# Transposing an expert tile's rows chunk by chunk, and cutting a scatter of rows into three pieces

## The chip, the cores and the metric

The kernel runs on one core of a Trainium2 chip. The metric is the device time of one execution in microseconds (us); lower is better. Each kernel is executed several times, and the median counts; one execution is also profiled, and all rows of the trace below come from that one.

## The reference

Three stages, all in float32, with batch 2, 8 heads, 576 positions, head size 64; 1152 tokens of 512 features; 8 experts of hidden size 1024; a last layer of hidden size 2048.

```
q_rot, k_rot = rotate(q), rotate(k)
attn = softmax(q_rot @ k_rot.T / 8)
x = (attn @ v) as [1152, 512]
logits = x @ w_gate + modality_bias[modality_id]
e_idx = argmax(logits);  gate_w = softmax(logits)[e_idx]
for e in range(8):
    mask = e_idx == e
    out[mask] = gate_w[mask] * (relu(x[mask] @ w1[e]) @ w2[e])
h = out @ w_in
out = (h * tanh(softplus(h))) @ w_out
```

## The kernel before, in words

**Products.** TensorE multiplies float32r operands. So that the result is as good as float32, each operand is kept as a high half (a rounded copy, made by ScalarE, ACT) and a low half (operand minus high half, made by VectorE, DVE, or GpSimd, POOL). Each product is three matmuls: high x high, high x low, low x high. For weights the halves are called `whi` and `wlo`, for tokens `xh` and `xl`, for the hidden layer `hh` and `hl`.

**Stages.** Attention fills the first 163 us. The expert stage follows up to 279 us, then the last layer. The batch has two halves, b = 0 and 1, of 576 tokens each. When attention for half b is done, `routing` (line 315) works out for each token its expert and its place among the rows sorted by expert. Then `scatters` (line 406) writes the half's rows from the tile `X` to `scratch` in DRAM: five indirect DMAs, one per tile of 128 (or 64) tokens, issued from POOL, each with a memset of a `spacer` behind it. Half 0's scatters are placed by a planner while attention still runs. Half 1's are issued in one go in the midst of its routing, since `routing` runs through them with `yield from scatters()` (line 422).

**Expert tiles.** The sorted rows of a half are worked off in tiles of T = 304 rows that belong to one expert: (0,0), (0,1), (1,0) and (1,1), with a loop for further tiles where an expert's rows don't fit, and which may run no times. `moe_tile` (line 681) handles one tile. Its weights come in eight chunks of 128 x 1024. `Feed.loads` (line 621) has SP load them ahead of use; `Feed.splits` (line 635) has ACT make a chunk's high half and POOL the low half, with a subtraction of about 2.4 us (line 611; chunk 4 of tile (0,0) goes to DVE). `Feed.ns` counts the chunks split so far. For f = 0 to 7, chunk f // 2 gives one block of the hidden layer with 12 matmuls; for d = 0 to 3, chunk 4 + d gives one block of the output with 24. The low halves of chunks 5, 6 and 7 of tile (0,0) appear in the trace as wlo(0, 0)_5, _6 and _7. The tags `whi` and `wlo` have three buffers each, so chunk n takes over that of chunk n - 3. A buffer of raw weights is free for SP's next load when POOL's subtraction has read it.

**Rows of the next tile.** At f = 3 SP loads the next tile's rows from `scratch`, as three row chunks of 128, 128 and 48 rows (`load_rows`, line 575); these loads wait until all scatters of their half have landed. At d = 0 ACT multiplies each row chunk by the gate (`moe_g`, line 645). Behind d = 1, `moe_x` (line 657) transposes the rows: for each of the four column chunks c it takes a PSUM bank, transposes the three row chunks into it, then ACT copies the bank to `xh` and DVE writes the difference to `xl`. Then the 48 matmuls of d = 2 and 3 follow, and the next tile. For tile (0,0) other code does this, inside attention (`x_tr`, line 1310), where the order is the planner's; `moe_x` serves tiles (0,1), (1,0) and (1,1). PSUM has seven banks in turn for this stage.

**The order of the work.** Each engine executes its own instructions in the order in which the program issues them, and this order is made by generators. `moe_tile` and what it calls yield a mark per instruction, with the engine's name and an estimated time. The loop at line 1473 runs half 1's routing and between its steps calls `pump` (line 1359), which advances the tiles by an allowance of TensorE's time; the allowance and two loads of the last layer's weights (`dl`) are chosen by the index of the routing's yield. Then `drive` (line 1451) runs the tiles on and, each 12 (later 7) yields of TensorE, issues one step of the decoding of the last layer's weights on DVE (lines 1401, 1406, 1411), up to a limit of 82 (72) steps.

```
        for i, y in enumerate(chain(route(1), merge_extra(nx))):
            if i in P["dl"]:
                dec_load(len(wr))
            if y[0] == "dve" or i == 8:
                pump(P["rq"][(i > 7) + (i > 8) + (i > 20)])
```

Of the kernel before, what the change touches and what calls it, by code (L numbers as in the profile page):

```python
# [10 lines left out]
F32 = mybir.dt.float32  # L11
F32R = mybir.dt.float32r
I32 = mybir.dt.int32
AF = mybir.ActivationFunctionType
ALU = mybir.AluOpType
# [10 lines left out]
T = 304  # L26
# [6 lines left out]
TCH = [(0, 128), (128, 128), (256, T - 256)]  # L33
KC = DM // 128
# [1 line left out]
FC2 = F2 // 128  # L36

Q = {'r0': 2.45, 'rd': 2.0, 'tanh': 1.06, 'rec': 1.1, 'hi': 2.2, 'lo': 2.38, 'o': 3.86}
P = {'sd': (4,), 'dl': (28, 44), 'qd': (2, 3), 'alt': (0.1, 4), 'd0': 82, 'vl': 24, 'w3': 3, 'rq': (0.2, 2.3, 0.55, 0.25), 'dec': (12, 7, 7), 'rl': 3, 'ah': 0, 'eps': 0.05, 'slack': 0.1}
K = {'ld': -22.67, 'prep': (-24.92, -22.38, -23.33, -27.14, -20.49, -7.62), 'sc': (-8.42, -3.18, 1.68, 1.67, 2.84, 10.44, 1.99, 8.05, 9.75), 'max': (-2.26, -5.46, -1.21, -1.85, 5.06, 8.41, 4.71, 11.42, 13.72), 'exp': (-3.19, 1.66, 6.32, 3.7, 13.26, 11.14, 14.6, -2.87, 25.74), 'tr': (0.69, 2.1, 2.56, 2.68, 5.53, 7.5, 8.45, 9.85, 10.88, 11.85, 15.56, 16.66, 16.92, 19.98), 'hi': (-3.91, -0.31, 2.51, 3.62, 4.25, 4.9, 5.01, 5.32, 7.26, 9.77, 13.56, 14.12, 14.6, 15.66), 'lo': (0.77, 1.83, 5.61, 6.34, 6.67, 7.32, 10.02, 10.73, 12.18, 13.92, 13.94, 14.62, 17.33, 18.02), 'pv': (7.08, 7.84, 10.5, 10.69, 14.13, 14.25, 14.32, 15.96, 18.04, 20.31, 21.03, 22.86, 23.97, 25.61), 'evac': (14.53, 9.65, 6.27, 25.13), 'rec': (-4.7, -0.45, 4.11, 12.71), 'fmm': (4.53, -3.79, 16.24, 17.22), 'norm': (15.5, 16.11, 26.18, 35.69)}  # L40

QT = [(0, 128), (128, 128), (256, 64), (320, 128), (448, 128)]
# [170 lines left out]
def moe_kernel(ctx: ExitStack, tc: tile.TileContext, aps, out):  # L213
    nc = tc.nc
# [95 lines left out]
    w4 = []  # L310
    tbl = {}
    scat, nxs, tes, tms = ([], []), [], [], []
    early = []

    def routing(b, bank):
        t = lambda sh, nm, dt=F32: rp.tile(sh, dt, tag=nm, name=f"{nm}{b}")
# [3 lines left out]
        def near(sh, nm):  # L320
# [19 lines left out]
            out=lg, in_=heads(X[b])[:, :, :, D:XW].rearrange("p j h e -> p j e h"),  # L340
# [15 lines left out]
            out=val, in0=lg, scalar=0.0, in1=iota8[:, 0:1, :].to_broadcast(sh),  # L356
# [12 lines left out]
        ps = bank()  # L369
# [5 lines left out]
        def scan():  # L375
# [8 lines left out]
            out=base[:, 1:], data0=ps[:, 0:n], data1=zero[:, :n],  # L384
# [8 lines left out]
            out=pos, in_=pz.rearrange("p (e j) -> p j e", j=5), axis=AX.X, op=ALU.add  # L393
# [9 lines left out]
        yield "dve", 0.12, True  # L403
        V.reciprocal(out=X[b][:, :, XC + 1], in_=sm8)

        def scatters():
            for j, (_, qn) in enumerate(QT):
                yield "pool", 1.25, False
                sc = nc.gpsimd.indirect_dma_start(
                    out=scratch,  # L410
                    out_offset=bass.IndirectOffsetOnAxis(ap=row[:qn, j:j + 1], axis=0),
                    in_=X[b][:qn, j], in_offset=None,
                )
                for o in scat[0] + scat[1]:
                    tc.declare_no_dep(sc.ins, o, reason="every token has a row of its own")
                for o in early if b else ():
                    tc.declare_no_dep(sc.ins, o, reason="rows of the other half")
                scat[b].append(sc.ins)
                nc.gpsimd.memset(spacer, 0.0)

        if b:
            yield from scatters()
        else:
            cur["scatters"] = scatters()
            yield "mark", 0.0, False
            side = False
# [11 lines left out]
            out=n1, in0=ce, scalar=float(T), in1=n0, op0=ALU.is_gt, op1=ALU.add  # L438
        )
        if side:  # L440
# [5 lines left out]
            out=qi, data0=n1, data1=zero[0:1, :NE], initial=0.0, op0=ALU.add, op1=ALU.add  # L446
# [7 lines left out]
            out=st, in0=s0, scalar=float(-T), in1=base[0:1, 0:n:5], op0=ALU.mult, op1=ALU.add  # L454
# [5 lines left out]
            out=nx, in0=qi[:, NE - 1:NE], scalar1=-2.0, scalar2=None, op0=ALU.add  # L460
        )
        tv = iotat[0:1, 0:ns]
        if b:
# [3 lines left out]
                out=tv[:, 0:2], in0=iotat[0:1, 0:2], scalar1=nx, scalar2=None, op0=ALU.add  # L467
# [3 lines left out]
                out=tv[:, 2:ns], in0=iotat[0:1, 2:ns], scalar1=nxs[0], scalar2=-2.0,  # L471
# [8 lines left out]
            out=lt, in0=qi[:, None, :].to_broadcast(s8),  # L480
            in1=tv[:, :, None].to_broadcast(s8), op=ALU.is_le,
# [9 lines left out]
            out=lt, in0=iota8[0:1, 0:1, :].to_broadcast(s8),  # L491
            in1=e8[:, :, None].to_broadcast(s8), op=ALU.is_equal,
# [8 lines left out]
            out=cs, in0=tv, scalar=float(T), in1=cs, op0=ALU.mult, op1=ALU.add  # L501
# [4 lines left out]
            out=tm[:, :, 1], in0=cs, scalar1=s1, scalar2=o1, op0=ALU.mult, op1=ALU.add  # L506
# [3 lines left out]
            out=tm[:, :, 1], in0=tm[:, :, 1], scalar1=0.0, scalar2=float(ROWS - T),  # L510
# [4 lines left out]
            out=tm[:, :, 0], in0=tm[:, :, 0], scalar1=float(NE - 1), scalar2=None, op0=ALU.min  # L515
# [98 lines left out]
    class Feed:  # L614
# [20 lines left out]
        def splits(self, n):  # L635
            while self.ns < min(n, self.nl):
                yield from split_chunk(*self.seq[self.ns])
                self.ns += 1
                yield from self.loads(0)

    xsplit, xpool = {}, []
# [15 lines left out]
    def moe_x(k, bank):  # L657

        if k not in gated:
            yield from moe_g(k)  # L660
        x = xrow.pop(k)
        pool = mp if k != "x" else xpool[0]
        xh = pool.tile([128, KC, T], F32R, tag="xh", name=f"xh{k}")
        xl = pool.tile([128, KC, T], F32R, tag="xl", name=f"xl{k}")
        for c in range(KC):
            yield "pe", 0.55, True
            ps = bank()
            for i, (r0, rn) in enumerate(TCH):
                nc.tensor.transpose(  # L669
                    out=ps[:, r0:r0 + rn], in_=x[:rn, i, c * 128:(c + 1) * 128],  # L670
                    identity=ident[:rn, :rn],
                )
            yield "act", 0.31, True
            nc.scalar.activation(out=xh[:, c], in_=ps[:, :T], func=AF.Copy)
            yield "dve", 0.39, True
            nc.vector.tensor_tensor(
                out=xl[:, c], in0=ps[:, :T], in1=xh[:, c].bitcast(F32), op=ALU.subtract
            )
        xsplit[k] = (xh, xl)

# [80 lines left out]
    def extra_tile(r):  # L761
# [4 lines left out]
        for _ in moe_x("x", cur["bank"]):  # L766
            pass
# [591 lines left out]
    def pump(x):  # L1359

        owed[0] += x
        while owed[0] > 0:
            y = next(gen0, None)
            if y is None:
                done0.append(1)
                return
            if y[0] == "pe":
                owed[0] -= y[1]
# [69 lines left out]
    with ExitStack() as mctx:  # L1438
# [34 lines left out]
        for i, y in enumerate(chain(route(1), merge_extra(nx))):  # L1473
            if i in P["dl"]:
                dec_load(len(wr))
            if y[0] == "dve" or i == 8:
                pump(P["rq"][(i > 7) + (i > 8) + (i > 20)])
        via[0] = cur["rtile"]
        drive(gen0, P["dec"][0], P["d0"], P["vl"])
        tile_rows(1)  # L1480
# [50 lines left out]
        def pool(name, bufs, **kw):  # L1531
# [4 lines left out]
        w2p, yp, gp, op = (  # L1536
            pool(n, b) for n, b in (("w2p", 1), ("yp", 1), ("gp", 3), ("op", 5))
        )
# [249 lines left out]
```

## Time and profile before

| what | us |
|---|---|
| median of three runs | 489.0 |
| the three runs | 492.23, 489.0, 488.71 |
| the profiled execution | 488.63 |
| its span, first to last instruction | 486.9 |

The span is what the trace covers; 1.7 us lie around it. In the rows, PE is TensorE's matmul, PEld its weight load, SPq the queue of SyncE, which issues most DMAs. A timeline row gives the start, the duration, the engine, the line, the operation with output and inputs, and the number of instructions in one row; in brackets the idle time of the engine before it and what ended it. Matmuls overlap: their durations are longer than the distance between their starts, and it is the starts that tell the pace.

### The profile page before, as it was taken

The numbers are of one execution on the slowest core, as the hardware profiler recorded it, in microseconds if no ns is written. First come the engines' busy times: TensorE is split into PE (matmuls) and PEld (weight loads), VectorE is DVE, ScalarE is ACT, GpSimd is POOL, SyncE is SP. The second block draws the span as 40 slices with busy tenths as digits, with TensorE's granted clock in tenths as the row PEclk, the third lists the DMA queues.
The fourth block names the chain that finished last, engine by engine and source line by source line (L and its number), as shares of the span: only waits on it lengthen the run. The fifth ranks groups of instructions, "written<-read, shape, count | busy, mean of one in ns | idle before, by whom it ended". The sixth has DMA issues, their size and how long they took to land.

```text
span 486.9 us, 8783 instructions
## 1 busy us (share of the span) xinstructions
PE 466.0 (96%) x2996; PEld 428.0 (88%) x2996; DVE 389.1 (80%) x616; ACT 332.5 (68%) x753; POOL 361.8 (74%) x363
## 2 busy tenths in 40 slices
PE   2799999999999989999999999999999999999995
PEld 1699999999989989999999998898989887888894
DVE  6698898899898665553878689999999859777773
ACT  3598888778878564574555487666676688776763
POOL 3799999999971697757756377877886749987654
PEclk9999999999999999999999999999999999999999
DMA  6789985877664598887974510012000001100002
GB/s 223 173 203 235 227 239 144 208 195 183 165 182 145 174 392 338 304 317 226 396 273 164 174 41 1 26 63 87 1 0 1 1 1 43 44 22 1 1 0 88
DMA packets 24131, 69.41 MB, mean 143 GB/s; under 512 B 5522, under 2 KB 9810, under 8 KB 22034
## 3 DMA queue, kind: packets, MB, share of 16 engines
q1 hardware_dynamic: 21794, 63.16, 41.9%
q0 software_dynamic: 1456, 5.03, 2.6%
q10 hardware_dynamic: 832, 0.61, 0.5%
q8 instruction: 25, 0.41, 0.4%
q14 instruction: 24, 0.20, 0.1%
HBM read 49.08 MB, written 6.44 MB: 114 GB/s over the span
## 4 chain that ended last, share of the span: by engine, by line
PE 52%; POOL 0%; issue 0%; ACT 0%; POOLq 0%; DVE 0%
PE h L1581 21%; PE o L1642 20%; PE mm L705 11%; PE mm L669 0%; POOL out_dram L1652 0%; POOLq L1784 0%; ACT ot L1648 0%; DVE yl L1519 0%; ACT yh L1517 0%; ACT Y L755 0%; POOL spacer L1659 0%; POOLq L1652 0%
## 5 line engine op out<-in xcount | busy, mean ns | idle before, releaser
L1607 DVE RECIPROCAL ta<-ta 128x320 f32<-128x320 f32 (+1 forms) x64 | 124.6, 1947 | 22.3 <-ACT ta L1600 20.8
L1555 POOL TENSOR_TENSOR w2l<-wc,w2h 128x512 fp32r<-128x512 f32 x64 | 90.3, 1432 | 16.4 <-ACT w2h L1554 8.3
L1642 PE MATMUL o<-w2h,g 128*128 128x512 f32 x288 | 97.7, 395 | 0.0
L1625 POOL TENSOR_TENSOR g<-ta,g 128x320 fp32r<-128x320 f32 (+1 forms) x63 | 51.7, 826 | 27.7 <-ACT g L1619 21.0
L972 PE MATMUL sc<-sk,sq 128*128 128x288 f32 (+1 forms) x320 | 59.4, 315 | 11.5 <-ACT sk L901 7.6
L1581 PE MATMUL h<-yl,w2h 128*128 128x320 f32 (+2 forms) x204 | 66.9, 328 | 0.1
L1581 PE MATMUL h<-yh,w2h 128*128 128x320 f32 (+2 forms) x204 | 66.9, 328 | 0.0
L1581 PE MATMUL h<-yh,w2l 128*128 128x320 f32 (+2 forms) x204 | 66.8, 328 | 0.0
L1642 PEld LDWEIGHTS o<-w2h,g 128*128 128x128 f32 x288 | 54.0, 188 | 11.6 <-POOL g L1625 0.2
L1007 ACT ACTIVATE pexp<-sc,nm 128x576 f32<-128x576 f32 x72 | 53.3, 741 | 15.5 <-DVE nm L996 11.7
L1040 ACT ACTIVATE ph<-pt 128x512 fp32r<-128x512 f32 (+2 forms) x112 | 54.8, 509 | 13.0 <-PE pt L1020 12.1
L996 DVE TENSOR_REDUCE nm<-sc 128x1 f32<-128x576 f32 x72 | 53.6, 752 | 10.8 <-PE sc L972 6.6
L972 PEld LDWEIGHTS sc<-sk,sq 128*128 128x128 f32 (+1 forms) x320 | 46.6, 190 | 14.2 <-ACT sk L901 7.9
L1642 PE MATMUL o<-w2l,g 128*128 128x512 f32 x144 | 56.8, 394 | 0.0
L1020 PE MATMUL pt<-ident,pexp 128*128 128x128 f32 (+1 forms) x360 | 54.5, 275 | 0.7 <-DVE tbl L521 0.6
L1061 PE MATMUL av<-ph,vhl 128*128 128x256 f32 (+1 forms) x160 | 50.7, 333 | 0.0
L1046 DVE TENSOR_TENSOR pl<-pt,ph 128x512 fp32r<-128x512 f32 (+1 forms) x80 | 48.7, 627 | 2.0 <-ACT ph L1040 1.8
L1596 ACT ACTIVATE ta<-h 128x320 f32<-128x320 f32 (+1 forms) x64 | 25.6, 401 | 30.7 <-PE h L1581 28.8
L1020 PEld LDWEIGHTS pt<-ident,pexp 128*128 128x128 f32 (+1 forms) x360 | 41.7, 136 | 3.5 <-issue 0.8
L1581 PEld LDWEIGHTS h<-yl,w2h 128*128 128x128 f32 x204 | 38.3, 188 | 4.1 <-DVE yl L1519 0.4
L1581 PEld LDWEIGHTS h<-yh,w2h 128*128 128x128 f32 x204 | 38.3, 188 | 3.9 <-DVE ta L1608 0.2
L1581 PEld LDWEIGHTS h<-yh,w2l 128*128 128x128 f32 x204 | 38.4, 188 | 2.3
(448 smaller groups left out, 1196.1 us busy)
## 6 DMA issues: line engine op xcount, KB each, us to landing
wr<-in_wio_dram SPq DMA_DIRECT2D x16, 1024.0 KB, 5.3
wc<-in_w_dram SPq DMA_DIRECT2D x26, 512.0 KB, 5.3
xs<-in_qk_dram SPq DMA_DIRECT2D x15, 576.0 KB, 5.3
sk<-ab SPq DMA_DIRECT2D x30, 288.0 KB, 4.1
sq<-ab SPq DMA_DIRECT2D x30, 144.0 KB, 2.4
vraw<-in_v_dram SPq DMA_DIRECT2D x16, 160.0 KB, 4.0
scratch<-zero SPq DMA_DIRECT2D x12, 108.8 KB, 5.0
xrow(0, 0)_2295<-scratch SPq DMA_DIRECT2D x2, 290.0 KB, 3.0
```

The lines of the kernel that those rows point to most:

```text
L705: nc.tensor.matmul(ps[:, :T], lhsT=w, rhs=m, start=(n == 0), stop=(n == 3 * len(pairs) - 1))
L972: nc.tensor.matmul(t[:m, hf, :NC2], lhsT=sq[:, c:c + m], rhs=sk[:, z, hf * NC2:(hf + 1) * NC2], start=(z == 0), stop=(z == 1),)
L996: nc.vector.tensor_reduce(out=nm[n, j], in_=sc[n, j][:, :, :NC2], axis=AX.XY, op=ALU.max, negate=True)
L1007: nc.scalar.activation(out=pe, in_=sc.pop((n, j))[:, :, :NC2], func=AF.Exp, bias=nm.pop((n, j)), accum_out=st[n, hf][:, i:i + 1],)
L1020: nc.tensor.transpose(out=t[:kn, o:o + 128], in_=pexp[n, j][:, k0:k0 + kn], identity=ident)
L1040: nc.scalar.activation(out=block(ph, n, hf, kts, slice(0, kn)), in_=psum(n, hf, kts, kn), func=AF.Copy)
L1061: nc.tensor.matmul(av[n, hf][:, :u.nq], lhsT=vhl[n][:, kt].rearrange("p a d -> p (a d)"), rhs=src[:, kt, u.at:u.at + u.nq], start=(kt == 0 ...
L1555: nc.gpsimd.tensor_tensor(out=lo[:, cs], in0=w[:, cs], in1=hi[:, cs].bitcast(F32), op=ALU.subtract)
L1581: nc.tensor.matmul(ps[:, :w], lhsT=wt[:, c], rhs=m[y][:, c], start=(n == 0), stop=(n == 11))
L1607: nc.vector.reciprocal(out=ta, in_=ta)
L1625: eng.tensor_tensor(out=gt[q][1][:, o:o + w], in0=tas.pop((q, i))[:, :w], in1=gt[q][0][:, o:o + w].bitcast(F32), op=ALU.subtract,)
L1642: nc.tensor.matmul(acc[g, t], lhsT=a[:, s], rhs=b, start=(f == 0 and z == 0), stop=(f == FC2 - 1 and z == 2),)
```

## The change

Two parts. In `moe_x` the loops are turned: row chunk by row chunk, each transposed for all four column chunks into four banks, then the four copies and differences. And half 1's scatters are issued as 0 to 2 where they were, 3 when six chunks have been split (behind chunk 5 of tile (0,0)), 4 when seven have. The indices that count the routing's yields are lowered by two.

```diff
-P = {'sd': (4,), 'dl': (28, 44), ...
+P = {'sd': (4,), 'ls': (6, 7), 'dl': (26, 42), ...
...
-    early = []
+    early, late = [], []
...
-        def scatters():
-            for j, (_, qn) in enumerate(QT):
+        def scatters(js=range(5)):
+            for j in js:
+                qn = QT[j][1]
                 yield "pool", 1.25, False
...
         if b:
-            yield from scatters()
+            yield from scatters(range(3))
+            late.extend(scatters([j]) for j in (3, 4))
...
                 yield from split_chunk(*self.seq[self.ns])
                 self.ns += 1
+                if self.ns in P["ls"]:
+                    yield from late.pop(0)
                 yield from self.loads(0)
...
-        for c in range(KC):
-            yield "pe", 0.55, True
-            ps = bank()
-            for i, (r0, rn) in enumerate(TCH):
+        ps = []
+        for i, (r0, rn) in enumerate(TCH):
+            yield "pe", (0.8, 0.8, 0.6)[i], True
+            for c in range(KC):
+                if i == 0:
+                    ps.append(bank())
                 nc.tensor.transpose(
-                    out=ps[:, r0:r0 + rn], in_=x[:rn, i, c * 128:(c + 1) * 128],
+                    out=ps[c][:, r0:r0 + rn], in_=x[:rn, i, c * 128:(c + 1) * 128],
                     identity=ident[:rn, :rn],
                 )
+        for c in range(KC):
             yield "act", 0.31, True
-            nc.scalar.activation(out=xh[:, c], in_=ps[:, :T], func=AF.Copy)
+            nc.scalar.activation(out=xh[:, c], in_=ps[c][:, :T], func=AF.Copy)
             yield "dve", 0.39, True
             nc.vector.tensor_tensor(
-                out=xl[:, c], in0=ps[:, :T], in1=xh[:, c].bitcast(F32), op=ALU.subtract
+                out=xl[:, c], in0=ps[c][:, :T], in1=xh[:, c].bitcast(F32), op=ALU.subtract
             )
...
-                pump(P["rq"][(i > 7) + (i > 8) + (i > 20)])
+                pump(P["rq"][(i > 7) + (i > 8) + (i > 18)])
```

## Rows read from the trace of the kernel before

**Rows 1.** The page's table of busy time: us, share of the span, instructions.

```profile
PE 466.0 (96%) x2996; PEld 428.0 (88%) x2996; DVE 389.1 (80%) x616; ACT 332.5 (68%) x753; POOL 361.8 (74%) x363
```

**Rows 2.** Waits of TensorE, 163 to 280 us: total, times, longest (all there are).

```profile
PE mm L705 <- POOL wlo(0, 0)_5_2744 L611: 1.2, 1, 1.2
PE mm L705 <- PEq L1493: 0.3, 1, 0.3
```

**Rows 3.** Timeline of TensorE at the first matmuls of chunk 5, tile (0,0).

```profile
180.10 0.30 PE L705 MATMUL mm<-hh(0, 0)_2571,whi(0, 0)_5_2742 128*128 128x304 f32 x1
180.24 0.30 PE L705 MATMUL mm<-hl(0, 0)_2572,whi(0, 0)_5_2742 128*128 128x304 f32 x1
181.76 0.41 PE L705 MATMUL mm<-hh(0, 0)_2571,wlo(0, 0)_5_2744 128*128 128x304 f32 x1 [1.22 <-POOL wlo(0, 0)_5_2744 L611]
182.01 0.30 PE L705 MATMUL mm<-hh(0, 0)_2571,whi(0, 0)_5_2742 128*128 128x304 f32 x1
```

**Rows 4.** Timeline of POOL: first and last of five scatters, two memsets, then wlo_5.

```profile
172.24 1.96 POOL L409 DMA_INDIRECT scratch<-X,row  x1
...
176.72 0.09 POOL L419 MEMSET spacer<- 1x1 f32 x1
...
178.29 0.97 POOL L409 DMA_INDIRECT scratch<-X,row  x1 [0.23 <-issue]
179.26 0.09 POOL L419 MEMSET spacer<- 1x1 f32 x1
179.32 2.39 POOL L611 TENSOR_TENSOR wlo(0, 0)_5_2744<-wc,whi(0, 0)_5_2742 128x1024 fp32r<-128x1024 f32 x1
```

**Rows 5.** Transposes of moe_x on TensorE: timelines, tile (0,1); busy time of three tiles.

```profile
184.95 2.25 PE L669 MATMUL mm<-ident,xrow(0, 1)_2628 128*128 128x128 f32 x12
187.12 0.41 PE L705 MATMUL mm<-hh(0, 0)_2571,whi(0, 0)_6_2792 128*128 128x304 f32 x1
...
185.06 0.46 PE L669 MATMUL mm<-ident,xrow(0, 1)_2628 128*128 128x128 f32 x2
...
185.26 0.52 PE L669 MATMUL mm<-ident,xrow(0, 1)_2628 48*128 48x48 f32 x2
...
185.45 0.44 PE L669 MATMUL mm<-ident,xrow(0, 1)_2628 128*128 128x128 f32 x2
...
sum 7.50, PE 6.73 PEld 4.27; mean PE 2.24 PEld 1.42
```

**Rows 6.** Timeline of TensorE in attention: transposes of tile (0,0), each with its successor.

```profile
155.35 0.45 PE L1312 MATMUL sc<-ident,xg(0, 0)_2423 48*128 48x48 f32 x4
155.73 0.41 PE L1020 MATMUL pt<-ident,pexp 128*64 128x128 f32 x2
...
159.15 0.93 PE L1312 MATMUL sc<-ident,xg(0, 0)_2423 128*128 128x128 f32 x7
159.95 0.33 PE L1091 MATMUL xo<-mov,avt 128*128 128x72 f32 x1
```

**Rows 7.** Timeline of TensorE: first readers of wlo_7 and of xl(0,1).

```profile
190.85 0.30 PE L705 MATMUL mm<-hh(0, 0)_2571,wlo(0, 0)_7_2845 128*128 128x304 f32 x1
...
194.05 0.30 PE L705 MATMUL mm<-xl(0, 1)_2923,whi(0, 1)_0_2948 128*128 128x304 f32 x1
```

**Rows 8.** Timeline of DVE: first decoding step after its wait, then xl(0,1).

```profile
185.92 0.70 DVE L1401 TENSOR_SCALAR rt<-wr 128x512 int32<-128x512 int32 x1 [6.00 <-DMA wr<-in_wio_dram]
...
187.99 1.61 DVE L676 TENSOR_TENSOR xl(0, 1)_2923<-mm,xh(0, 1)_2922 128x304 fp32r<-128x304 f32 x4
```

**Rows 9.** Timeline of ACT: the gates of tile (1,0).

```profile
208.74 1.94 ACT L651 ACTIVATE xrow(1, 0)_3073<-xrow(1, 0)_3073 128x512 f32<-128x512 f32 x3
```

**Rows 10.** Timeline of SP (two rows); landing of half 1's five scatters.

```profile
182.11 0.45 SPq L1385 DMA_DIRECT2D wr<-in_wio_dram  x1
...
195.85 1.46 SPq L580 DMA_DIRECT2D xrow(1, 0)_3073<-scratch  x3
...
DMA to landing us min/median/max: 7.6/8.3/8.4
```

More of the change, by code (lines that the diff above doesn't have):

```diff
@@ L38 @@
 Q = {'r0': 2.45, 'rd': 2.0, 'tanh': 1.06, 'rec': 1.1, 'hi': 2.2, 'lo': 2.38, 'o': 3.86}
-P = {'sd': (4,), 'dl': (28, 44), 'qd': (2, 3), 'alt': (0.1, 4), 'd0': 82, 'vl': 24, 'w3': 3, 'rq': (0.2, 2.3, 0.55, 0.25), 'dec': (12, 7, 7), 'rl': 3, 'ah': 0, 'eps': 0.05, 'slack': 0.1}
+P = {'sd': (4,), 'ls': (6, 7), 'dl': (26, 42), 'qd': (2, 3), 'alt': (0.1, 4), 'd0': 82, 'vl': 24, 'w3': 3, 'rq': (0.2, 2.3, 0.55, 0.25), 'dec': (12, 7, 7), 'rl': 3, 'ah': 0, 'eps': 0.05, 'slack': 0.1}
 K = {'ld': -22.67, 'prep': (-24.92, -22.38, -23.33, -27.14, -20.49, -7.62), 'sc': (-8.42, -3.18, 1.68, 1.67, 2.84, 10.44, 1.99, 8.05, 9.75), 'max': (-2.26, -5.46, -1.21, -1.85, 5.06, 8.41, 4.71, 11.42, 13.72), 'exp': (-3.19, 1.66, 6.32, 3.7, 13.26, 11.14, 14.6, -2.87, 25.74), 'tr': (0.69, 2.1, 2.56, 2.68, 5.53, 7.5, 8.45, 9.85, 10.88, 11.85, 15.56, 16.66, 16.92, 19.98), 'hi': (-3.91, -0.31, 2.51, 3.62, 4.25, 4.9, 5.01, 5.32, 7.26, 9.77, 13.56, 14.12, 14.6, 15.66), 'lo': (0.77, 1.83, 5.61, 6.34, 6.67, 7.32, 10.02, 10.73, 12.18, 13.92, 13.94, 14.62, 17.33, 18.02), 'pv': (7.08, 7.84, 10.5, 10.69, 14.13, 14.25, 14.32, 15.96, 18.04, 20.31, 21.03, 22.86, 23.97, 25.61), 'evac': (14.53, 9.65, 6.27, 25.13), 'rec': (-4.7, -0.45, 4.11, 12.71), 'fmm': (4.53, -3.79, 16.24, 17.22), 'norm': (15.5, 16.11, 26.18, 35.69)}
```

## The prediction, made blind

> **What bounds the kernel now.** I read four views, from wide to narrow. First the page's table of busy time: TensorE is busy for 466.0 of 486.9 us [rows 1], so little can be won except by giving it less to do or by closing a gap in it. Then TensorE's waits in the expert stage, 163 to 280 us: there are two in the whole stage, 1.2 us for one low half of weights, wlo(0,0)_5, that POOL makes late, and 0.3 us at a branch [rows 2]. Then the timeline on both sides of the first wait. On TensorE the second matmul of chunk 5 starts at 180.24, the third only at 181.76 [rows 3]. On POOL the reason is in sight: five scatters of half 1 stand in one row from 172.24 to 179.35, and wlo(0,0)_5 is the next instruction behind them [rows 4]. Last, the transposes of a tile's rows: twelve of them hold TensorE from 184.95 to 187.12, 0.18 us each [rows 5], while the transposes of tile (0,0), which stand in the attention stage with their 48-row pieces together, go at less than that [rows 6]. So TensorE sets the end, and both parts of the change touch its own queue.
>
> **Part 1: the scatters in pieces.** Two ordinary matmuls of this shape start 0.14 us apart (180.10 and 180.24). Without the wait the third would stand at 180.38; it stands at 181.76, 1.38 us late, and the step behind it, to 182.01, is 0.25 instead of 0.14, another 0.11 [rows 3]. The pause therefore costs 1.49 us, not the 1.2 us of the waits view.
>
> After the change POOL issues scatters 0 to 2, then wlo_5, scatter 3, wlo_6, scatter 4, wlo_7. The memset behind scatter 2 ends at 176.81. wlo_5 starts at once (it followed the last memset so before) and takes 2.39 us: ready at 179.2 instead of 181.7 [rows 4]. Its high half is there: TensorE used it at 180.10 [rows 3]. TensorE asks at 180.38, so 1.2 us are to spare and the whole 1.49 us goes. What is late next? Scatter 3 starts some 0.2 us behind wlo_5 and takes 0.97 like the last one before; with its memset it ends at 180.5, so wlo_6 is ready at 182.9. Scatter 4 puts wlo_7 at 184.2 to 186.6 [rows 4]. TensorE read wlo_6 two matmuls behind 187.12 and wlo_7 at 190.85 [rows 5, 7]; less 1.49 and the 0.82 of part 2 that is 185.1 and 188.5. Both have about 2 us of cover. A scatter in this stretch took 0.97 to 1.96 us [rows 4]. With 1.96 for each late one, wlo_7 is ready at 188.6, a cost of 0.1 us at most. I take 0.97, since the 1.96 is one of five and stood beside a DVE subtraction, while DVE is idle from 179.92 to 185.92 [rows 8].
>
> What else moves: SP's next weight load waits for wlo_5 and stands in front of the second decoder load at 182.11 [rows 10]; both leave 2.5 us earlier. Scatters 3 and 4 end on POOL about 2.4 and 4.8 us later than before; they land 7.6 to 8.4 us after issue [rows 10], so the last row is in place near 192. The row load of tile (1,0) waits for it on SP; it ran at 195.85 [rows 10] and will be due near 193.5. That is 1.5 us of cover. Should it fail, the rows are wanted only by ACT's gates at 208.74 less 2.3 [rows 9], 13 us later; a landing as slow as the scatters' leaves another 4 us.
>
> The shifted indices (26, 42 and 18 for 28, 44 and 20) count two scatter yields less and name the same points of the routing: nothing.
>
> **Part 2: row chunk by row chunk.** The rows of narrow windows give the steps from one transpose's start to the next: 128 rows behind 128 rows 0.11 (184.95 to 185.06), 48 rows behind 128 0.20 (to 185.26), 128 behind 48 0.19 (to 185.45) [rows 5]. Four such groups make the 2.17 us. A change of the row count is what costs: eight of the twelve steps are such changes (the last one leads to the next matmul). The new order has eight pieces of 128 rows, then four of 48: two changes.
>
> The sum: seven steps of 0.11 are 0.77; one of 0.20; then four of 48 rows with the way out. The attention stage has just that: from 155.35 to the next instruction at 155.73, 0.38 us [rows 6]. It also has seven of 128 rows in 0.80 us, 0.114 a step. Together 1.35 instead of 2.17: 0.82 us saved per tile. Three tiles pass through this code, with twelve transposes and the same busy time each (6.73 us for three) [rows 5] ((0,0) is done by other code): 2.46 us.
>
> Bounds: if each 48-row step costs the 0.20 of a change, it is 0.77 + 0.80 + 0.19 = 1.76, a saving of 0.41 per tile, 1.2 in all. The new order also changes the PSUM bank at each step instead of each third. If that alone made every step 0.20, it would be 11 x 0.20 + 0.19 = 2.39, a loss of 0.22 per tile, 0.7 in all. The four of 155.35 also went to four banks, and took 0.38 us with the way out, so I take 0.82. Nothing speaks for less than 0.11 on the 128-row steps.
>
> The Trainium skill ("TensorE: Matmul & The Clock Gate", section LDWEIGHTS) says that a weight load's time goes by its columns, not its rows, so that a 32-row load lasts as long as a 128-row one, some 107 ns for 128 columns. By that the three steps among the 48-row pieces would be 0.107 us each, 0.13 us more per tile than the sum above has. The trace goes against it: four such pieces in 0.38 us with the way out [rows 6].
>
> The copies out of PSUM begin later: ACT's first behind the ninth transpose instead of the third, about 0.7 us, then four in a row. They and DVE's four differences are wanted by the next tile's first matmuls, 48 matmuls or 6.7 us behind the transposes; xl was started at 187.99 and read at 194.05 [rows 7, 8]. Four banks at once were also live before, out of seven; the fourth takes over the bank of a product evacuated long before. The function yields three times for TensorE instead of four, so the decoding steps on DVE, counted in such yields, slip by one to three matmuls (0.4 us); their number by the stage's end stays, since limits cap it. No matmul of this stage waits for DVE [rows 2], so: nothing.
>
> **The sum.** 1.49 + 2.46 = 3.95 us. The profiled execution took 488.63 with a span of 486.9; 488.63 - 3.95 = 484.7. The median shown is 489.0, 0.4 above that execution, so on its scale 485.0. Behind the expert stage TensorE runs without a gap that is not its own, so what is won there arrives at the end.
>
> **Rivals** (times on the median's scale, 489.0).
>
> A, the array's steps don't shrink as in the attention stage (bank changes or 48-row steps at the price of a change): between a loss of 0.7 and a gain of 1.2; with the pause closed that is 486.3 to 488.2, say 487.2. For it: the order in attention was not quite this one. Against: all kinds of step are in the rows.
>
> B, the pause only moves from wlo_5 to wlo_6 or wlo_7, since the late scatters run slow (1.96 and more): 489.0 - 2.46 = 486.5. It needs over 1 us per scatter beyond the usual.
>
> C, the 48-row pieces follow each other at the 0.11 of the 128-row ones, since both load 128 columns: 0.77 + 0.20 + 0.33 + 0.19 = 1.49 per tile, 3 x 0.14 = 0.4 us less gained, 485.4. Against it stands the row of four [rows 6]. (The rule of the page named above would lead here.)
>
> D, the other side: the loads that wlo_5 releases earlier collide with decoder weights already under way. DVE stands until 185.92 for these [rows 8], and the differences xl(0,1) stand behind its decoding. xl(0,1)'s first piece was begun at 187.99 [rows 8], so ready at 188.5; TensorE wanted it at 194.05 [rows 7] and will at 191.7. From 3.2 us of delay each further microsecond is TensorE's; over 3.2 + 3.95 = 7.2 us the kernel is slower than it was; with 9 us, half as much again as DVE's whole wait of 6.00, it is 485.0 + 5.8 = 490.8. Against: the bytes under way are the same, and two loads of 1.5 MB leaving 2.5 us earlier can hardly take more than about 1.2 us of the others' time (half of 2.5, an estimate).
>
> **How the numbers follow.** Chances: forecast 0.69, A 0.10, B 0.10, C 0.07, D 0.04. The forecast's own range is 484.2 to 486.0 (0.1 to 0.2% of scatter on such runs). The range reaches over C and B and half of A: 484.0 to 487.6. About 1%, 4.9 us, is what a measurement of this kernel can tell from no change. The forecast, 0.8%, lies short of it: faster by over 1% 0.20 (the runs' own scatter must help), within 1% 0.77, slower by over 1% (the far end of D) 0.03.
>
> **What would show it.** Right: TensorE's waits no longer name wlo(0,0)_5; POOL shows scatter, wlo_5, scatter, wlo_6, scatter, wlo_7; the twelve transposes take about 1.35 us to the next matmul, the 48-row ones four in a row; tile (1,0) starts about 3.1 us earlier, the first product of the last stage 3.9 us earlier. Wrong: a wait for wlo(0,0)_6 or _7 or for xl(0,1) on TensorE, transposes still over 1.8 us, an ACT gate that waits for rows, or an earlier start of the last stage that is lost again before the end.

## The result, and the profile after

The kernel after takes 485.3 us (median of six, 485.0 to 485.4) against 488.9 in the runs of before beside it: a ratio of 0.9916, interval 0.9892 to 0.9939. One of the six runs of before took 492.23 us, the others 488.71 to 489.25; by the medians alone the gain is 3.6 us and the ratio 0.9926. The forecast was 485.0 us. The profiled execution took 485.32 us with a span of 483.6, so 3.3 us less than the profiled one of before, where the sum had said 3.95. TensorE is busy 1.8 us less [rows 1], and of its waits in the expert stage the one for wlo(0,0)_5 is gone. The page's table of busy time, then TensorE's waits, 163 to 280 us as in [rows 2] (here from 155 on; the first row is attention's):

```profile
PE 464.2 (96%) x2996; PEld 427.7 (88%) x2996; DVE 390.4 (81%) x616; ACT 331.2 (68%) x753; POOL 361.9 (75%) x363
```

```profile
PE xo L1098 <- ACT avt L1077: 0.5, 1, 0.5
PE mm L712 <- PEq L1500: 0.3, 1, 0.3
```

(Lines stand one to seven further down in the kernel after: L409 is L410, L611 is L613, L669 is L675, L705 is L712.) POOL's timeline shows the order of the change. wlo_5 starts where the third scatter's memset ends; it is ready at 179.35, and TensorE uses it at 180.66, with no pause. POOL's rows, then TensorE's:

```profile
172.41 1.97 POOL L410 DMA_INDIRECT scratch<-X,row  x1 [0.15 <-issue]
...
175.97 0.92 POOL L410 DMA_INDIRECT scratch<-X,row  x1 [0.22 <-issue]
176.88 0.09 POOL L420 MEMSET spacer<- 1x1 f32 x1
176.94 2.41 POOL L613 TENSOR_TENSOR wlo(0, 0)_5_2740<-wc,whi(0, 0)_5_2738 128x1024 fp32r<-128x1024 f32 x1
179.51 0.99 POOL L410 DMA_INDIRECT scratch<-X,row  x1 [0.17 <-issue]
...
180.56 2.41 POOL L613 TENSOR_TENSOR wlo(0, 0)_6_2792<-wc,whi(0, 0)_6_2790 128x1024 fp32r<-128x1024 f32 x1
183.13 0.98 POOL L410 DMA_INDIRECT scratch<-X,row  x1 [0.17 <-issue]
...
184.18 2.39 POOL L613 TENSOR_TENSOR wlo(0, 0)_7_2845<-wc,whi(0, 0)_7_2843 128x1024 fp32r<-128x1024 f32 x1
```

```profile
180.52 0.30 PE L712 MATMUL mm<-hl(0, 0)_2572,whi(0, 0)_5_2738 128*128 128x304 f32 x1
180.66 0.31 PE L712 MATMUL mm<-hh(0, 0)_2571,wlo(0, 0)_5_2740 128*128 128x304 f32 x1
180.81 0.30 PE L712 MATMUL mm<-hh(0, 0)_2571,whi(0, 0)_5_2738 128*128 128x304 f32 x1
```

The transposes of tile (0,1) [rows 5] take 183.73 to 185.07, 1.34 us to the next matmul instead of 2.17. TensorE's timeline, with a row of a narrower window between, which shows the four 48-row pieces in one run:

```profile
183.73 1.41 PE L675 MATMUL mm<-ident,xrow(0, 1)_2628 128*128 128x128 f32 x12
...
184.69 0.45 PE L675 MATMUL mm<-ident,xrow(0, 1)_2628 48*128 48x48 f32 x4
...
185.07 0.41 PE L712 MATMUL mm<-hh(0, 0)_2571,whi(0, 0)_6_2790 128*128 128x304 f32 x1
```

Step by step, from the starts of the twelve in the trace: 128 rows behind 128 go at 0.109 us, the first 48-row piece follows at 0.203, the next three at 0.099, 0.061 and 0.063, and the matmul behind them at 0.153. All three tiles are alike; the windows view of line 675 (PE busy, its count, weight loads, clock, DMA share, GB/s):

```profile
183.73:185.06 1.33, 1.33 (x12) 1.12 (x11) 1.00 1.03 419
211.90:213.23 1.33, 1.33 (x12) 1.12 (x11) 1.00 1.10 431
240.60:241.93 1.33, 1.33 (x12) 1.12 (x11) 1.00 0.97 403
```

Where the time came from and where some went again is read best by stage: how long from the first matmul of the expert stage to the first transpose of tile (0,1), how long to the first product of the last layer, and from there to the end of the span. TensorE's timeline, first before, then after:

```profile
162.89 0.38 PE L705 MATMUL mm<-xh(0, 0)_2502,whi(0, 0)_0_2371 128*128 128x304 f32 x1
...
279.17 0.31 PE L1581 MATMUL h<-yh,w2h 128*128 128x320 f32 x1
```

```profile
163.17 0.39 PE L712 MATMUL mm<-xh(0, 0)_2502,whi(0, 0)_0_2371 128*128 128x304 f32 x1
...
275.45 0.31 PE L1588 MATMUL h<-yh,w2h 128*128 128x320 f32 x1
```

To the first transpose it is 22.06 us before and 20.55 after, 1.50 less, which is part 1. The whole expert stage is 116.28 before and 112.27 after, 4.01 less; of the other 2.51, the transposes of the three tiles make 2.49, which is part 2. From there to the end it is 207.74 before and 208.16 after, 0.42 more. And attention had let the stage begin 0.28 later. 4.01 - 0.42 - 0.28 = 3.31, the difference of the spans.

**The 0.42 us in the last layer.** TensorE stops there once, in front of the third product of line 1649. Counted from the layer's first product, the matmuls ahead of this one start as in the kernel before, within 0.06 us; this one starts 0.32 us later, the next 0.43, and nothing further is lost. The weight-load row of the kernel after, whose bracket names the wait, and around it TensorE's row:

```profile
356.52 0.40 PE L1649 MATMUL o<-w2l,g 128*128 128x512 f32 x1
357.07 0.73 PE L1649 MATMUL o<-w2h,g 128*128 128x512 f32 x2
...
357.07 0.30 PEld L1649 LDWEIGHTS o<-w2h,g 128*128 128x128 f32 x2 [0.58 <-POOL g L1632]
```

POOL's g (the last layer's activated hidden block) stands behind DVE's reciprocals, and DVE is busy for 51.28 of the 52 us from 305 to 357. What made DVE late lies at 331 us. The timelines of DVE and POOL there, before:

```profile
333.55 1.26 DVE L1728 CAST idi<-idf 128x9 int32<-128x9 f32 x1
334.72 1.21 DVE L1411 SCALAR_TENSOR_TENSOR wc<-wr,wc 128x1024 int32<-128x1024 int32 x1
335.86 2.14 DVE L1607 RECIPROCAL ta<-ta 128x320 f32<-128x320 f32 x1
...
333.48 3.61 POOL L1555 TENSOR_TENSOR w2l<-wc,w2h 128x512 fp32r<-128x512 f32 x2
```

and after:

```profile
329.82 1.26 DVE L1735 CAST idi<-idf 128x9 int32<-128x9 f32 x1
331.00 2.39 DVE L1418 SCALAR_TENSOR_TENSOR wc<-wr,wc 128x1024 int32<-128x1024 int32 x1
333.31 2.14 DVE L1614 RECIPROCAL ta<-ta 128x320 f32<-128x320 f32 x1
...
329.75 2.55 POOL L1562 TENSOR_TENSOR w2l<-wc,w2h 128x512 fp32r<-128x512 f32 x2
```

The reader is to see an exchange. The same decoding step takes 1.21 us before and 2.39 after. POOL's two subtractions beside it take 3.61 together before and 2.55 after. The cast in front, of nine elements a partition, takes 1.26 us in both: as long as POOL's first subtraction still runs. When that ends, DVE's step and POOL's second subtraction are both due (their starts in the trace are 12 ns apart before and 18 after), and one of the two takes a subtraction longer than the other. Before, this was POOL, which had slack; after, it was DVE, which had none. From this step on, counted again from the layer's first product, DVE's instructions start 1.18 to 1.19 us later than before, and POOL's from 336 us on 1.18 to 1.20, up to the g for which TensorE stops. The 1.18 us that DVE lost reach TensorE as this stop; the rest is cover that TensorE had, since before this g had ended 0.9 us ahead of the matmul that reads it. It is not the clock: from 305 to 357 us it was granted at 1.00 in both executions.

The Trainium skill ("SBUF — State Buffer", section Who interferes with whom) says that a DVE instruction with two SBUF inputs contends with a GpSimd instruction that reads SBUF, that the lock is exclusive, and that the order of issue decides who is blocked. The rows agree as to the lock (DVE's step 1.21 against 2.39 us, POOL's two subtractions 3.61 against 2.55). As to the order they show less: DVE's start is recorded first in both executions, and it lost in one.

### The profile page after: what moved, and what is told of

It reads as the page before. It is cut to its first block, busy times and chain, and to the rows that moved or that the text cites. A ratio compares the mean times of both kernels' runs of the same rounds, so it can differ in the third digit from the quotient of the medians.

```text
span 483.6 us, 8783 instructions
## 1 busy us (share of the span) xinstructions
PE 464.2 (96%) x2996; PEld 427.7 (88%) x2996; DVE 390.4 (81%) x616; ACT 331.2 (68%) x753; POOL 361.9 (75%) x363
## 4 chain that ended last, share of the span: by engine, by line
PE 41%; DVE 8%; issue 3%; POOL 1%; ACT 1%; POOLq 0%; DVEq 0%; ACTq 0%
PE h L1588 15%; PE o L1649 15%; PE mm L712 11%; DVE ta L1614 6%; DVE wc L1418 1%; DVE ta L1615 1%; POOL out_dram L1659 0%; DVE wc L1408 0%; PE mm L675 0%; DVE wc L1413 0%; POOLq L1791 0%; POOL g L1632 0%; DVE idi L1735 0%; ACT ot L1655 0%; DVE yl L1526 0%
## 5 line engine op out<-in xcount | busy, mean ns | idle before, releaser
L1562 POOL TENSOR_TENSOR w2l<-wc,w2h 128x512 fp32r<-128x512 f32 x64 | 89.3, 1417 | 15.3 <-ACT w2h L1561 15.3
L1632 POOL TENSOR_TENSOR g<-ta,g 128x320 fp32r<-128x320 f32 (+1 forms) x63 | 52.7, 841 | 27.9 <-ACT g L1626 21.3
L1626 ACT ACTIVATE g<-ta 128x320 fp32r<-128x320 f32 (+1 forms) x64 | 27.9, 436 | 22.9 <-DVE ta L1615 22.5
```

The costliest lines, as they stand in the source:

```text
L1562: nc.gpsimd.tensor_tensor(out=lo[:, cs], in0=w[:, cs], in1=hi[:, cs].bitcast(F32), op=ALU.subtract)
L1632: eng.tensor_tensor(out=gt[q][1][:, o:o + w], in0=tas.pop((q, i))[:, :w], in1=gt[q][0][:, o:o + w].bitcast(F32), op=ALU.subtract,)
```

## The experiments

Each kernel ran beside runs of the kernel before. Those beside the parts alone, the first profile of the mixed order and the cast moved in the kernel after had a median of 489.17 us, those beside the others 489.51, so the ratios are to be compared, not the times. The theory: the change's two parts add up by the prediction's sum (a pause of POOL's making, and a price for each change of the row count), and the 0.42 us come from the exchange between DVE and POOL. The rivals: the bank order or the pieces' size makes the transposes slow; the parts cover each other; the last layer loses because it begins earlier.

### One part alone

The order of the transposes alone (the kernel after, with all five scatters in a row and the indices as before):

```diff
-            yield from scatters(range(3))
-            late.extend(scatters([j]) for j in (3, 4))
+            yield from scatters()
```

> Only the new order of the transposes; half 1's five scatters in one row as before. My theory (the two parts are independent and add): the wait for wlo(0,0)_5 stays, 1.2 us in the waits view and 1.5 in all; the twelve transposes take 1.34 us to the next matmul instead of 2.17 at all three tiles; the last layer's first product starts 2.5 us earlier than before, and the time is 486.4. Rival (the parts overlap, one of them alone brings most): 485.3 to 485.8.

The scatters alone (the kernel after, with the loops of `moe_x` as before):

```diff
-        for i, (r0, rn) in enumerate(TCH):
-            yield "pe", (0.8, 0.8, 0.6)[i], True
-            for c in range(KC):
...
+        for c in range(KC):
+            yield "pe", 0.55, True
+            ps = bank()
+            for i, (r0, rn) in enumerate(TCH):
```

> Only the scatters in three pieces; the transposes column chunk by column chunk as before. My theory: no wait for wlo(0,0)_5 and none for _6 or _7; transposes 2.17 us; the last layer's first product 1.5 us earlier than before, time 487.4. Rival (the parts overlap): 485.3 to 486.

Measured: the order alone 486.59 us, ratio 0.9949 (0.9934 to 0.9963), which is 2.5 us; the scatters alone 487.7 us, ratio 0.9974 (0.9965 to 0.9984), 1.3 us. By the ratios the two make 3.8 and the whole change 4.1 (0.84%); by the medians it is 2.6 and 1.5 against 3.6. They add up as far as the intervals can tell, and neither came near the 485.3 to 486 of the rival. The expert stage tells it more finely (table below): 2.70 and 1.57 us shorter, 4.01 for the whole change, and 0.18 of the 2.70 belongs to a pause that was shorter in that execution. In the trace of the order alone the wait is back, in TensorE's waits and in its timeline:

```profile
PE mm L711 <- POOL wlo(0, 0)_5_2744 L612: 1.0, 1, 1.0
```

```profile
180.49 0.30 PE L711 MATMUL mm<-hh(0, 0)_2571,whi(0, 0)_5_2742 128*128 128x304 f32 x1
180.63 0.30 PE L711 MATMUL mm<-hl(0, 0)_2572,whi(0, 0)_5_2742 128*128 128x304 f32 x1
181.97 0.41 PE L711 MATMUL mm<-hh(0, 0)_2571,wlo(0, 0)_5_2744 128*128 128x304 f32 x1 [1.04 <-POOL wlo(0, 0)_5_2744 L612]
182.22 0.30 PE L711 MATMUL mm<-hh(0, 0)_2571,whi(0, 0)_5_2742 128*128 128x304 f32 x1
```

Here the pause costs (181.97 - 180.63 - 0.14) + (182.22 - 181.97 - 0.14) = 1.31 us, against 1.49 in [rows 3]: TensorE would have used wlo_5 at 180.77, 0.39 later than in [rows 3], and POOL began it at 179.53, only 0.21 later than in [rows 4]; 1.49 - 0.18 is the 1.31. So the term of part 1 is not a constant. It is what POOL is late by in an execution. The two timed kernels that have part 1 alone (the scatters alone, and the mixed order below) put it at 1.3 by their ratios, 1.4 to 1.5 by their medians.

### What makes a transpose slow

The kernel after, with the row chunks in turn, 128, 128, 48, and each transpose to another bank than the one before it:

```diff
-        for i, (r0, rn) in enumerate(TCH):
-            yield "pe", (0.8, 0.8, 0.6)[i], True
-            for c in range(KC):
...
+        ps = [bank() for _ in range(KC)]
+        for s in range(12):
+            if s % 4 == 0:
+                yield "pe", (0.8, 0.8, 0.6)[s // 4], True
+            c, i = s % KC, s % 3
```

> The changed kernel with the twelve transposes in another order: 128, 128, 48 rows in turn as before, but each into another bank than the one ahead of it. My theory (the change of the row count is the price, not the bank): 2.17 us to the next matmul, as before the change; time 1.49 below before, or 487.4 to 487.8. Rival (three transposes in one bank in a row are the price): 1.35 us as in the changed kernel, 485.3.

Measured, a single execution: 490.21 us, more than either expected value. The twelve transposes took 2.17 us at each tile, as the theory has it. But the expert stage had begun at 166.01, some 2.8 us later than in the kernel after. The reason stands in front of everything that was edited: POOL had waited 2.1 us for an input load, and behind it DVE and TensorE waited too. The two rows, POOL's and TensorE's timeline:

```profile
130.21 2.65 POOL L924 TENSOR_TENSOR xs<-xs,tabs 128x1152 f32<-128x1152 f32 x1 [2.06 <-DMA xs<-in_qk_dram]
...
135.67 0.55 PE L1027 MATMUL pt<-ident,pexp 128*128 128x128 f32 x3 [2.14 <-DVE pl L1053]
```

Whether the new order had brought this was to be settled by more executions of the same kernel.

> The same kernel as e4_mixed (128, 128 and 48 rows in turn, each transpose to the next bank), timed in rounds. In its one look the transposes took 2.17 us to the next matmul, as in the kernel before, but TensorE had also stood still for 2.1 us at 133 us, in the attention stage, for a DVE reciprocal behind an input load that landed late. Theory (only changes of the row count cost): this stop was of that execution alone; without it the kernel keeps part 1's gain and has nothing of part 2's: about 487.6 us (487.2 to 488.0), with 2.17 us at each of three tiles and no stop at 133 us. Rival (the mixed order itself moves the stage ahead of it and costs 2 us): 489.8 to 490.4 again, with the stop at 133 us there again.

Measured: 488.15 us (487.88 to 488.58), ratio 0.9973 (0.9963 to 0.9983), which is what the scatters alone gave (0.9974); on the scale of the first group that is 487.8. The stop at 133 us is not there. Of line 675 the windows view shows, tile by tile, the price of before:

```profile
184.33:186.49 2.16, 2.16 (x12) 1.28 (x11) 1.00 1.07 436
213.34:215.49 2.15, 2.15 (x12) 1.28 (x12) 1.00 1.00 411
242.87:245.03 2.16, 2.16 (x12) 1.28 (x11) 1.00 0.84 337
```

A new bank with each transpose costs as much as a new bank with each third one (2.17 us both), and nothing in the kernel after. What costs is a change between 128 and 48 rows. The step over it takes 0.19 to 0.20 us (0.15 where the four 48-row pieces lead to the next matmul), and the step behind it is longer too: 0.164 to 0.169 instead of 0.109 among 128-row pieces, 0.099 instead of 0.06 among 48-row ones. The old order and the mixed one have eight changes in twelve steps, the new one two. Two starts of tile (0,1) in the kernel before show such a step behind a change, from the 185.45 of [rows 5] to 185.62, and the next change:

```profile
185.62 0.27 PE L669 MATMUL mm<-ident,xrow(0, 1)_2628 128*128 128x128 f32 x1
...
185.82 0.26 PE L669 MATMUL mm<-ident,xrow(0, 1)_2628 48*128 48x48 f32 x1
```

TensorE's weight loads show where much of it goes. The loads of the 128-row pieces begin one piece ahead: in the kernel after, the first at 183.59 for its matmul at 183.73. The load of a 48-row piece behind a 128-row one begins only together with its own matmul, after 0.17 us without a load. Waits of the weight loads at these lines, 182 to 250 us, before, after and in the mixed order; then, of the kernel after, the loads of tile (0,1) as a group (shortest, median and longest in ns) and the four 48-row ones in the timeline:

```profile
PEld mm L669 <- issue: 2.0, 12, 0.2
```

```profile
PEld mm L675 <- issue: 0.5, 3, 0.2
```

```profile
PEld mm L675 <- issue: 2.0, 12, 0.2
```

```profile
L675 PEld LDWEIGHTS mm<-ident,xrow(0, 1)_2628 x12: 136/140/145, 183.6 to 184.9; 128*128 128x128 f32 x8, 48*128 48x128 f32 x4
```

```profile
184.69 0.32 PEld L675 LDWEIGHTS mm<-ident,xrow(0, 1)_2628 48*128 48x128 f32 x4 [0.17 <-issue]
```

The nine pauses that are gone are 1.5 of the 2.49 us of part 2. The Trainium skill ("TensorEngine Tiling (Array Packing)", section Key Properties) says that a change of the tiling mode drains TensorE. It gives no price, and whether going from 128 to 48 rows is such a change no row shows: the pauses would fit it, and the cause of the price stays open.

### How late POOL may be

The kernel after, with four scatters in front of wlo_5 and one behind it, and the indices that count the yields one higher:

```diff
-            yield from scatters(range(3))
-            late.extend(scatters([j]) for j in (3, 4))
+            yield from scatters(range(4))
+            late.extend(scatters([j]) for j in (4,))
```

> After, but with four scatters in a row ahead of wlo(0,0)_5 and only one behind it. One scatter with its memset takes 1.27 us on POOL, so wlo(0,0)_5 should start at about 178.2 instead of 176.94 us and be ready at 180.6; TensorE asks for it at about 180.8. Theory (the pause is what POOL is late by, with a threshold): no wait or at most 0.2 us, transposes at 1.34 us; the time of after, 485.3 us (485.0 to 485.7). Rival (each scatter that stands ahead costs its share of the pause, some 0.7 us for this one, since two of the five were moved for 1.49 us): a wait of about 0.7 us for wlo(0,0)_5 and 486.0 us.

Measured: 485.47 us, ratio 0.9915 (0.9898 to 0.9931), the time of after. The waits view names no wait for wlo(0,0)_5, and the steps in TensorE's timeline are 0.18 and 0.24 around the matmul that asks, instead of 0.14 and 0.14, so 0.14 us in all:

```profile
181.29 0.30 PE L712 MATMUL mm<-hl(0, 0)_2572,whi(0, 0)_5_2740 128*128 128x304 f32 x1
181.47 0.41 PE L712 MATMUL mm<-hh(0, 0)_2571,wlo(0, 0)_5_2742 128*128 128x304 f32 x1
181.71 0.30 PE L712 MATMUL mm<-hh(0, 0)_2571,whi(0, 0)_5_2740 128*128 128x304 f32 x1
```

POOL had begun wlo_5 at 179.00 and ended it at 181.41, just when TensorE came. So one scatter moved does nearly what two do, and the pause has a threshold: a scatter ahead of wlo_5 costs nothing until POOL is late. The rival's 0.7 us a scatter did not come.

### The exchange in the last layer

The kernel after, with the cast of the output's row numbers, which stood in front of the decoding step, moved behind unit 34:

```diff
-        at2(16.2, nc.vector.tensor_copy, idi, idf)
+        at2(34.0, nc.vector.tensor_copy, idi, idf)
```

> The changed kernel, and the cast of the row numbers (1.26 us of DVE at 330) is issued some 70 us later, where DVE rests. My theory of the missing 0.4 us: the last layer's DVE has no slack from 305 to 357 us, and one decoding step lost a race for a port to POOL by nanoseconds and took 2.39 instead of 1.21 us. With the cast gone from that stretch DVE has 1.2 us of slack again: TensorE's pause at 357 goes, time 484.9, 0.4 below the changed kernel. Rival (the 0.4 us belong to TensorE's clock, mean 0.998 in that profile, or to the run): 485.3, as the changed kernel.

The same edit in the kernel before:

> The kernel before, with the one change of e3: the copy of the output's row numbers to integers stands behind unit 34 of the last layer instead of unit 16. Theory (in the kernel before the third decoding step got the port ahead of POOL, 1.21 us, and DVE was not late for TensorE there): nothing to win, 488.9 us (488.6 to 489.3), span 486.8. Rival (the cast's place costs TensorE time by itself, whoever gets the port): 0.3 us or more less, 488.6 us and below, and a first product of output at unit 34 that comes earlier against the first product of the layer.

And the kernel after, with one tiny instruction on POOL that gives DVE the lead:

```diff
+                if q == 9 and c:
+                    nc.gpsimd.memset(spacer, 0.0)
                 nc.gpsimd.tensor_tensor(
                     out=lo[:, cs], in0=w[:, cs], in1=hi[:, cs].bitcast(F32), op=ALU.subtract
                 )
```

> After, with one more memset of one element on POOL (0.09 us) ahead of the second half of the low weights of unit 9 in the last layer. In after that subtraction and DVE's third decoding step start 18 ns apart at 331.0 us, and DVE's step takes 2.39 us; in the kernel before they start 12 ns apart and POOL's takes 2.35. Theory (whoever gets to the shared port first runs at 1.2 to 1.3 us, and the other waits for it): DVE's step starts clearly first and takes 1.21 us, POOL's takes 2.2 to 2.4; DVE keeps its 1.18 us, TensorE does not stop at 357 us for POOL's g, and the span is 0.3 to 0.4 us shorter than after's 483.6: 483.2, a time of 484.9. Rival (the 0.4 us were lost because everything comes 3.7 us earlier than some transfer or DVE can follow): DVE's step may shorten, but TensorE still stops some 0.4 us at 357 us; 485.3 us.

Measured: the cast later 485.17 us (484.98 to 486.96), ratio 0.9928 (0.9914 to 0.9942); the same in the kernel before 489.63 us, ratio 1.0002 (0.9992 to 1.0011); the memset on POOL 485.71 us, ratio 0.9920 (0.9904 to 0.9937). No time differs from that of the same kernel without the edit by as much as the runs scatter. The 484.9 us that was expected of the cast later and of the memset came in neither, and 0.4 us are too little to be seen so; the argument rests on the traces. With the memset, DVE's step has its 1.21 us and POOL's subtraction waits (timelines of DVE and POOL):

```profile
331.80 1.21 DVE L1418 SCALAR_TENSOR_TENSOR wc<-wr,wc 128x1024 int32<-128x1024 int32 x1
...
331.79 0.09 POOL L1563 MEMSET spacer<- 1x1 f32 x1
331.84 2.33 POOL L1564 TENSOR_TENSOR w2l<-wc,w2h 128x512 fp32r<-128x512 f32 x1
```

and TensorE's stop at 357 us is gone. That the memset brought this, one trace cannot show: without it DVE won in four of seven. All ten traces on one table, by stage (from the first matmul of the expert stage to the first product of the last layer, and from there to the end of the span), with the decoding step that stands behind the cast and the longest wait of TensorE's weight loads for POOL's g between 300 and 400 us:

| trace | expert stage, us | last layer, us | DVE's step, us | TensorE waits for g, us |
|---|---|---|---|---|
| before | 116.28 | 207.74 | 1.21 | none |
| after | 112.27 | 208.16 | 2.39 | 0.6 |
| order alone | 113.58 | 207.73 | 1.21 | none |
| scatters alone | 114.72 | 208.13 | 2.40 | 0.5 |
| mixed order, single execution | 114.72 | 207.77 | 1.21 | none |
| mixed order, timed | 114.81 | 207.88 | 2.39 | 0.6 |
| four scatters and one | 112.42 | 207.74 | 1.21 | none |
| after, memset on POOL | 112.30 | 207.74 | 1.21 | none |
| after, cast later | 112.28 | 207.70 | 2.30 (no cast ahead) | none |
| before, cast later | 116.20 | 207.75 | 2.31 (no cast ahead) | none |

Where the cast stood ahead, TensorE stopped wherever DVE's step took 2.4 us, and nowhere else. With the cast moved, the step was slow too, but DVE had been spared the cast's 1.26 us, and TensorE did not stop: so what counts is how late DVE gets. It isn't the earlier start of the layer: four kernels with 112.3 to 112.4 us in the expert stage stand in the table, and only one of them lost. Nor is it the kernel: the mixed order is the same program in both of its rows, and it won once and lost once. Behind the stop TensorE was 0.41 to 0.43 us late in all three. At the end of the span the loss was 0.14 to 0.42: in the timed mixed order 0.27 us of it came back further on, for a reason that was not looked into.

## Why the prediction was right, point by point

The mechanism of both parts came as it was forecast, and so did their sizes: 4.01 us in the expert stage for a sum of 3.95. What was not forecast is that the profiled spans differ by 0.70 us less than that (3.31 us).

**Part 1.** Forecast 1.49 us, measured 1.50 in the two profiled executions, and some 1.3 by the times of the kernels that have it alone. wlo_5 was ready at 179.35 (forecast 179.2), wlo_6 at 182.97 (182.9), wlo_7 at 186.57 (186.6); both late scatters took 0.98 to 0.99 us, so the 0.97 was the right one of the two bounds. TensorE read wlo_7 at 188.79 (188.5), 2.2 us behind its end. Rival B, a pause that moves on, did not come.

**Part 2.** Forecast 1.35 us to the next matmul and 0.82 saved per tile, measured 1.34 and 0.83; three tiles give 2.49 us for a forecast of 2.46. The steps among 48-row pieces are 0.099, 0.061 and 0.063, and 0.153 leads out of them: 0.376 for a forecast of 0.38. Rival A falls with these steps, and its bank changes with the mixed order too; rival C (0.11 for a 48-row piece) falls with these steps. One reading in the prediction is off: "Four such groups make the 2.17 us" does not come out, since four times 0.11, 0.20 and 0.19 are 2.00. The other 0.17 is the step behind a change, 0.164 to 0.169 in three of the four groups. The forecast did not hang on it: the 2.17 was measured as a whole, and the new order's steps were taken from runs of equal pieces. The prediction also weighed the Trainium skill ("TensorE: Matmul & The Clock Gate", section LDWEIGHTS), by which a weight load's time goes by columns, not rows. The loads in the trace agree: all twelve of tile (0,1) last 0.136 to 0.145 us, whatever their rows, and longer than the 0.107 that the prediction worked out. But they overlap, four of them in 0.32 us, so a load's time is not the step, which was 0.06 us among 48-row pieces and 0.11 among 128-row ones, and to read the rule as a step of 0.107 us goes beyond what it says.

**What moves beside it.** The row load of tile (1,0) ran at 193.81 (forecast 193.5), its gates at 206.68 (206.4), the differences xl(0,1) at 187.12, read at 191.99 (191.7). No ACT gate waits, and no matmul waits for xl. DVE's longest wait for decoder weights went down to 4.96 us from 6.00 [rows 8]; in sum it waited 9.6 us for them between 163 and 280 us, against 8.0 before, which no matmul felt: rival D did not come.

**The step that failed.** "Behind the expert stage TensorE runs without a gap that is not its own, so what is won there arrives at the end." No row stands beside it in the prediction, though it held for TensorE as it ran before, which was busy for all of the 52 us from 305 to 357. It left out that DVE has 0.7 us to spare in 52 us of the last layer, and that one of its steps falls due together with a POOL instruction that can hold it up. 0.42 of 4.01 us was given back there in the profiled execution. The other 0.28 us by which the spans differ less than the stages came ahead of the change: the same attention code let the expert stage begin between 162.9 and 164.0 us in all traces but the two in which an input load came late. Neither was in the sum; together they are 0.70 us, and the forecast's own range, 484.2 to 486.0, had room for them.

## What to carry to other kernels

Put pieces of one shape next to each other on TensorE: here a step between 128 and 48 rows cost some 0.09 us more than one between equal 128-row pieces, and the step behind it another 0.04 to 0.06. The saving could be counted from the starts in the trace of before, to 0.01 us a tile. A wait for an engine that comes late has a threshold, so move the least that passes it, and leave the rest: here one scatter moved left 0.14 us of the pause, two left none. Before you say that a gain arrives at the end, look for the stretch behind it where another engine is busy all the time, and at what can hold that engine up; and compare executions stage by stage, since what comes in front of the change moves by as much as its last tenths.

## What was not expected of the hardware

The contest between DVE and POOL falls either way from one execution of a program to the next. In the eight traces with the cast ahead the decoding step and the subtraction start 2 to 39 ns apart, DVE always first in the record; five times DVE had 1.21 us, three times 2.39 or 2.40. The largest lead, 39 ns, is that of the memset. Below it the lead does not decide: DVE won with 2, 12, 14 and 16 ns and lost with 10, 16 and 18. What does, the records don't show, and that stays open.

A cast of nine elements a partition took 1.26 us beside POOL's subtraction, and 0.19 to 0.20 us at its later place, where an instruction of POOL had 0.16 to 0.17 us left to run. In both it ended some 0.03 us behind POOL's.

An input load of the attention stage can land 2 us late, and the execution is then 2 to 3 us longer; it did so in the traces of two kernels: besides the mixed order's single execution it struck the profiled execution of the kernel before with the cast moved, which took 492.81 us where its median is 489.63. There TensorE stood still for 2.29 us up to 135.38, and its granted clock was then at the lower level, 0.50 (1.2 GHz), from 136.12 to 139.53 us; in the other, behind a stop of 2.14 us, it stayed at 1.00. POOL's timeline there, and that stretch in the windows view (busy time of PE, PEld, DVE, ACT and POOL, then clock, DMA share, GB/s):

```profile
129.91 2.66 POOL L917 TENSOR_TENSOR xs<-xs,tabs 128x1152 f32<-128x1152 f32 x1 [2.15 <-DMA xs<-in_qk_dram]
```

```profile
136.12:139.53 3.41, 3.41 (x18) 3.39 (x15) 3.35 (x10) 2.64 (x7) 2.98 (x5) 0.50 0.67 147
```
